# Head pairs split two ways in a chunked RWKV-7 recurrence, half-height state products, and the feed-forward tail moved a chunk later

## The chip, the cores and the metric

The kernel runs on one core of one Trainium2 chip. The metric is the device time of one execution in microseconds (us), as the median of several executions. This program uses one core, so no comparison between the two halves of the chip is needed: every execution quoted here was recorded as a fast one, with its span and its mean granted TensorE clock. The engines are PE (TensorE, matrix products; its weight loads are listed apart as PEld), DVE (VectorE), ACT (ScalarE), POOL (GpSimd) and SP (SyncE, which here only starts transfers).

## The reference, cut to what matters

Four batches of eight heads run a recurrence over 768 steps, with a 40 by 40 state per head. Its output, 3072 tokens of 320 numbers, goes through a feed-forward network (FFN) with a squared ReLU.

```python
B, H, S, D = 4, 8, 768, 40
for t in range(S):                                   # per batch and head
    y[t] = r[t] @ state
    Sa = state @ a[t]
    state = state * w[t][None, :] - outer(Sa, b[t]) + outer(v[t], k[t])
x = y.transpose(0, 2, 1, 3).reshape(3072, 320)
h = np.maximum(x @ w_in, 0.0)                        # w_in  320 x 2048
out = (h * h) @ w_out                                # w_out 2048 x 320
```

## The kernel before

Time is cut into 12 chunks of 64 steps. Inside a chunk the recurrence becomes matrix products: the scaled `a` against the scaled `k` and `b` gives triangular 64 by 64 squares (`PNT`), `r` against the corrected `v` and `b` gives others (`CXT`). `G0` and `M` are two steps of solving the triangular system, `S` is the state that goes to the next chunk, and `ST` is its transpose. `Y` is the chunk's output, and it feeds the FFN of that chunk while the next chunk's recurrence runs. Matrix inputs are bf16, sums are fp32 in PSUM.

All instructions are issued in program order on each engine (`manual_schedule`), so the order of the calls in the loop is the schedule. Three tags: `tr`, one PSUM buffer that every group of transposes shares; `acc`, one buffer for all state and pair products; `hp`, two buffers for the FFN's first product (and for the cumulative sums `cs`).

```python
def transposes(srcs, dst, eng):                       # t_r, t_kb, t_a, t_vm
    trp = ps.tile([128, 8, 128], BF16, name="trp", tag="tr", bufs=1)
    for i, s in enumerate(srcs):
        nc.tensor.transpose(out=trp[:, i, :], in_=s, identity=IDb[:])
    if eng == "act":
        nc.scalar.activation(out=dst, in_=trp[:], func=ACTF.Copy)
    else:
        nc.vector.tensor_copy(out=dst, in_=trp[:])

def scale(self, key, dst, fac):                       # scale_b, scale_k, scale_a
    nc.vector.tensor_tensor(out=dst[:, :, 0:D], in0=self.nat[key][:],
                            in1=fac[:].rearrange("p (h e) -> p h e", e=D), op=ALU.mult)

def state_term(self, bp, acc, lhsT, rhs):             # full height, K = 128
    for q in range(4):
        g = 4 * bp + q
        mm(acc[:, q, 0:160], lhsT[:, g, :], rhs(g), q % 2 == 0)

def g0(self, bp):
    acc = self.acc[bp] = self.new_acc()               # tag "acc", bufs=1
    if not self.first:
        self.state_term(bp, acc, self.AT, ...)        # against ST
    self.pairs(bp, acc, self.PNT[bp], self.VM, not self.first)
    self.evac_m(bp, acc, self.G0)                     # two ACT copies with scale -1

def t_s(self, bp):
    trs = ps.tile([128, 4, 2, 128], BF16, name="trs", tag="tr", bufs=1)
    ...                                               # 8 transposes of S, 2 copies to ST

def t_x(self):
    ...                                               # 6 transposes of Y, tag "tr"
    nc.vector.tensor_copy(out=self.XT[:], in_=trx[:])

def ffn_in(self, jj):                                 # 6 matmuls, then
    ...
    nc.scalar.activation(out=hs[:], in_=hp[:], func=ACTF.Relu)
    nc.vector.tensor_tensor(out=self.Gt[:, 2 * jj:2 * jj + 2, :], in0=hs[:],
                            in1=hs[:], op=ALU.mult)

# the loop (cur: this chunk, nxt: the next, prv: the one before); cut: guards, loads of r and v
for c in range(NCH):
    cur.g0(0); nxt.cs(0); nxt.cs(1); prv.t_x(); nxt.gamp()
    cur.m(0); nxt.t_r(); nxt.scale_b(); nxt.scale_k(); nxt.decays()
    prv.ffn_in(0); prv.ffn_in(1)
    cur.state(0); cur.t_vm(0); nxt.scale_a(); load(c + 2, ...)
    prv.ffn_in(2); cur.g0(1); prv.ffn_in(3)
    cur.t_s(0); cur.m(1); nxt.spread(); prv.ffn_in(4); prv.ffn_in(5)
    cur.state(1); cur.t_vm(1); prv.ffn_in(6); cur.cx(0); prv.ffn_in(7)
    nxt.t_kb(0); cur.y(0); cur.t_s(1); prv.ffn_out(0, 0); cur.cx(1)
    nxt.t_kb(1); prv.ffn_out(0, 1); cur.y(1); nxt.t_a()
    prv.ffn_out(1, 0); nxt.pn(0); prv.ffn_out(1, 1); nxt.pn(1); ch[c + 2].ln()
```

Between two groups of transposes there are nearly always FFN matmuls (`ffn_in`, `ffn_out`) or squares (`cx`). They need nothing from the transposes, so PE has work while another engine empties the one `tr` buffer.

Of the kernel before, what the change touches and what calls it, by code (L numbers as in the profile page):

```python
# [14 lines left out]
def kernel(  # L15
# [11 lines left out]
):  # L27

# [40 lines left out]
    MASK = gl.tile([128, 8, L], BF16, name="MASK")  # L69
    nc.vector.memset(MASK[:], 1.0)  # L70
    for half in range(2):
        nc.gpsimd.affine_select(
            out=MASK[64 * half:64 * half + 64], in_=MASK[64 * half:64 * half + 64],
            pattern=[[0, 8], [1, L]],
            compare_op=ALU.is_gt, fill=0.0, base=0, channel_multiplier=-1,
        )
# [9 lines left out]
    G0s = pair("G0", [128, 2, NI, 64], BF16)  # L86
    Ss = pair("S", [128, NG, 2, 2, 64], BF16)
    STs = pair("ST", [128, NG, 2, 2, D], BF16)
# [5 lines left out]
    def fixed_values(i):  # L94


        for t_ in (Bps[i], Kps[i], Rps[i], Aps[i]):
            nc.vector.memset(t_[:, :, D:64], 0.0)
        for b2 in range(2):
            vrow = 64 - 64 * b2  # L100
            nc.vector.memset(VMs[i][vrow:vrow + 64, b2, :, D:64], 0.0)
            nc.vector.memset(G0s[i][vrow:vrow + 64, b2], 0.0)
        nc.vector.memset(STs[i][:], 0.0)
        nc.vector.memset(Ss[i][:], 0.0)
        nc.vector.memset(Ys[i][:, 640:704], 0.0)

    def load_weights():
        nc.vector.memset(WIN[64:128, 2, :], 0.0)
        nc.gpsimd.dma_start(out=WIN[:, 0:2, :],
                            in_=moe_w_in[0:256, :].rearrange("(g p) f -> p g f", p=128))  # L110
        nc.gpsimd.dma_start(out=WIN[0:64, 2, :], in_=moe_w_in[256:320, :])
        nc.gpsimd.dma_start(out=WOUT[:], in_=moe_w_out.rearrange("(j p) f -> p j f", p=128))
# [42 lines left out]
    class Chunk:  # L155


        def __init__(self, c):
# [6 lines left out]
            self.S, self.ST = Ss[1 - i], STs[1 - i]  # L165
            self.Sn, self.STn = Ss[i], STs[i]
            self.PNT, self.CXT, self.VMT, self.acc = {}, {}, {}, {}
# [24 lines left out]
        def decays(self):  # L192
# [4 lines left out]
            self.GLr = pr.tile([128, 2, W_], BF16, name="GLr", tag="GLr")  # L197
# [5 lines left out]
        def spread(self):  # L203
            for b2 in range(2):
                nc.gpsimd.dma_start(out=self.GLr[0:64 + D, b2, :],  # L205
                                    in_=self.gld[b2:b2 + 1, :].to_broadcast([64 + D, W_]))

        def scale(self, key, dst, fac):
            nc.vector.tensor_tensor(out=dst[:, :, 0:D], in0=self.nat[key][:],
                                    in1=fac[:].rearrange("p (h e) -> p h e", e=D),  # L210
                                    op=ALU.mult)
# [33 lines left out]
        def squares(self, lhs_of, rhs_of, dst):  # L245

            pq = [ps.tile([128, 4, 2, L], FP32, name=f"sq{p}", tag=f"sq{p}", bufs=1)
                  for p in range(2)]
            for q in range(4):
                for b2 in range(2):  # L250
                    for p in range(2):
                        mm(pq[p][:, q, b2, :], lhs_of(q, b2, p), rhs_of(q, b2, p), True)
            dv = dst[:].rearrange("s (q p) b t -> s q p (b t)", p=2)
            for p in range(2):
                nc.vector.tensor_tensor(  # L255
                    out=dv[:, :, p, :], in0=pq[p][:].rearrange("s q b t -> s q (b t)"),
                    in1=MASK[:].rearrange("s (q b) t -> s q (b t)", b=2), op=ALU.mult)

        def pn(self, bp):
            self.PNT[bp] = wk.tile([128, 8, 2, L], BF16, name="PNT", tag="PNT")  # L260
            g0 = 4 * bp
            self.squares(lambda q, b2, p: self.KBT[64 * p:64 * p + D, b2, g0 + q, :],
                         lambda q, b2, p: self.AT[64 * p:64 * p + D, g0 + q,
                                                  64 * b2:64 * b2 + 64],
                         self.PNT[bp])

        def cx(self, bp):
            self.CXT[bp] = wk.tile([128, 8, 2, L], BF16, name="CXT", tag="CXT")
            g0 = 4 * bp
            self.squares(lambda q, b2, p: self.VMT[bp][64 * p:64 * p + D, q, b2, :],  # L270
                         lambda q, b2, p: self.RT[64 * p:64 * p + D, g0 + q,
                                                  64 * b2:64 * b2 + 64],
                         self.CXT[bp])

        def new_acc(self):
            return ps.tile([128, 4, 256], FP32, name="acc", tag="acc", bufs=1)

        def pairs(self, bp, acc, lhs, rhs, started):
            for i in range(8):
                q, p = divmod(i, 2)  # L280
                mm(acc[:, q, 80 * p:80 * p + 80], lhs[:, i].rearrange("s b t -> s (b t)"),
                   rhs[:, :, 8 * bp + i, 0:D], not started and i % 4 == 0)

        def state_term(self, bp, acc, lhsT, rhs):
            for q in range(4):
                g = 4 * bp + q
                mm(acc[:, q, 0:160], lhsT[:, g, :], rhs(g), q % 2 == 0)

        def evac_m(self, bp, acc, dst):
            for b2 in range(2):  # L290
                rows = slice(64 * b2, 64 * b2 + 64)
                src = acc[rows, :, 0:160].rearrange("s q (p b d) -> s q p b d", p=2, b=2)
                nc.scalar.activation(  # L293
                    out=dst[rows, b2, 8 * bp:8 * bp + 8, 0:D].rearrange(
                        "s (q p) d -> s q p d", p=2),
                    in_=src[:, :, :, b2, :], func=ACTF.Copy, scale=-1.0)

        def g0(self, bp):
            acc = self.acc[bp] = self.new_acc()
            if not self.first:  # L300
                self.state_term(bp, acc, self.AT,
                                lambda g: self.ST[:, g].rearrange("k p b d -> k (p b d)"))
            self.pairs(bp, acc, self.PNT[bp], self.VM, not self.first)
            self.evac_m(bp, acc, self.G0)

        def m(self, bp):
            self.pairs(bp, self.acc[bp], self.PNT[bp], self.G0, True)
            self.evac_m(bp, self.acc[bp], self.VM)

        def state(self, bp):  # L310
            if self.last:
                return
            accs = self.new_acc()
            VM, KB, g0 = self.VM, self.KB, 4 * bp
            if not self.first:
                for j in range(2):
                    mm(accs[:, 2 * j:2 * j + 2, 0:160], IDb[:],
                       self.S[:, g0 + 2 * j:g0 + 2 * j + 2, :, :, 0:D].rearrange(
                           "s g b p d -> s (g b p) d"), True)
            for q in range(4):  # L320
                for b2 in range(2):
                    g = g0 + q
                    mm(accs[:, q, 80 * b2:80 * b2 + 80], VM[:, b2, 2 * g:2 * g + 2, :],
                       KB[:, b2, 2 * g:2 * g + 2, 0:D],
                       self.first and q % 2 == 0 and b2 == 0)
            for p in range(2):
                rows = slice(64 * p, 64 * p + D)
                ai = accs[rows, :, 0:160].rearrange("s q (b p d) -> s q b p d", p=2, b=2)
                gv = self.GLr[rows].rearrange("s b (g p d) -> s g b p d", g=NG, p=2)
                nc.vector.tensor_tensor(out=self.Sn[rows, g0:g0 + 4, :, p, 0:D],  # L330
                                        in0=ai[:, :, :, p], in1=gv[:, g0:g0 + 4, :, p],
                                        op=ALU.mult)

        def t_s(self, bp):
            if self.last:
                return
            trs = ps.tile([128, 4, 2, 128], BF16, name="trs", tag="tr", bufs=1)
            g0 = 4 * bp
            for q in range(4):
                for b2 in range(2):  # L340
                    nc.tensor.transpose(  # L341
                        out=trs[:, q, b2, :],
                        in_=self.Sn[:, g0 + q, b2].rearrange("s p d -> s (p d)"),
                        identity=IDb[:])
            for p in range(2):
                rows = slice(64 * p, 64 * p + 64)
                nc.vector.tensor_copy(out=self.STn[rows, g0:g0 + 4, p],
                                      in_=trs[rows, :, :, 64 * p:64 * p + D])

        def t_vm(self, bp):  # L350
            self.VMT[bp] = wk.tile([128, 4, 2, 128], BF16, name="VMT", tag="VMT")
            g0 = 4 * bp
            transposes([self.VM[:, b2, 2 * (g0 + q):2 * (g0 + q) + 2, :]
                        for q in range(4) for b2 in range(2)],
                       self.VMT[bp][:].rearrange("s q b t -> s (q b) t"), "dve")

        def y(self, bp):
            accy = self.new_acc()
            if not self.first:
                self.state_term(bp, accy, self.RT,  # L360
                                lambda g: self.S[:, g, :, :, 0:D].rearrange(
                                    "k b p d -> k p b d"))
            self.pairs(bp, accy, self.CXT[bp], self.KB, not self.first)
            for b2 in range(2):
                rows = slice(64 * b2, 64 * b2 + 64)
                src = accy[rows, :, 0:160].rearrange("s q (p b d) -> s q p b d", p=2, b=2)
                cols = slice(320 * bp, 320 * bp + 320)
                v4 = lambda x: x.rearrange("s (q p d) -> s q p d", q=4, p=2)
# [4 lines left out]
        def t_x(self):  # L373
# [7 lines left out]
            nc.vector.tensor_copy(out=self.XT[:], in_=trx[:])  # L381
            self.Gt = wk.tile([128, NJ, 256], BF16, name="Gt", tag="Gt")

        def ffn_in(self, jj):
# [8 lines left out]
            hs = wk.tile([128, 2, 256], BF16, name="hs", tag="hs", bufs=3)  # L393
# [147 lines left out]
```

## Time and profile before

| | before |
|---|---|
| time, median of 2 runs | 339.66 us (339.51 to 339.81) |
| span in the profile | 338.2 us |
| a steady chunk | 24.35 us |
| PE at work per steady chunk | 21.63 us |
| DVE, ACT at work per steady chunk | 19.43, 14.84 us |
| PE waiting per steady chunk | 2.71 us |

The steady chunk is read from the timeline. The line below appears once in each chunk, so the distance between two of its starts is the time of one chunk. The columns are start, duration of the group, engine, line, operation, output and inputs, count, and in brackets the idle time just before with what ended it.

```profile
136.64 0.89 DVE L185 TENSOR_TENSOR CSE<-cs,lnW 128x320 f32<-128x320 f32 x2 [0.76 <-ACT GAMI L183]
...
160.96 0.89 DVE L185 TENSOR_TENSOR CSE<-cs,lnW 128x320 f32<-128x320 f32 x2 [0.76 <-ACT GAMI L183]
```

The second line starts 24.32 us after the first; over eight chunks, from 87.98 to 282.75 us, the mean is 194.77 / 8 = 24.35 us (seven of them take 24.32 to 24.34, one 24.46).

Over the whole span the page's first part has PE at work 80% of the time, DVE 71% and ACT 53%. The table of windows for the eight steady chunks alone is more useful, since start and end have other limits. The kernel before; the columns are the stretch, its length, then busy time and instructions of PE, PEld, DVE, ACT and POOL, the granted PE clock, the share of the DMA engines and GB/s.

```profile
87.98:282.75 194.77, 173.06 (x2420) 138.87 (x2418) 155.45 (x288) 118.73 (x209) 73.37 (x88) 1.00 0.90 115
```

PE is at work 173.06 of 194.77 us, 89%; it idles 21.71 us, 2.71 us a chunk. The list of PE's waits in the same eight chunks of the same kernel tells whom it waits for (in total, how often, the longest):

```profile
PE trp L145 <- DVE XT L381: 7.3, 8, 0.9
PE acc L152 <- DVE CXT L255: 4.5, 16, 0.4
PE acc L152 <- DVE S_96 L330: 3.9, 4, 1.1
PE acc L152 <- DVE S_97 L330: 3.8, 4, 1.0
PE trp L145 <- DVE VMT L149: 1.6, 8, 0.2
```

These five add up to 21.1 of the 21.71 us. The last of them: PE needs the `tr` buffer that the VMT copy on DVE empties, and it waits 0.2 us each time. The timeline of that place, before:

```profile
146.42 0.61 PE L145 MATMUL trp<-IDb,VM_92 128*128 128x128 bf16 x8
...
147.22 0.99 DVE L330 TENSOR_TENSOR S_96<-acc,GLr 40x320 bf16<-40x320 f32 x2
...
147.96 0.83 PE L389 MATMUL hp<-XT,WIN 128*128 128x256 bf16 x6
148.24 0.69 DVE L149 COPY VMT<-trp 128x1024 bf16<-128x1024 bf16 x1
...
148.99 0.61 PE L145 MATMUL trp<-IDb,KB 128*128 128x128 bf16 x8 [0.20 <-DVE VMT L149]
```

PE writes `tr` at 146.42. DVE first does the two S multiplies, which stand ahead in its order, and then the VMT copy, although the transposes that the copy reads ended at 147.03. So `tr` is free at 148.93. That takes 2.57 us from one group of transposes to the next, but PE fills it with two FFN groups and the squares of `cx(0)` (from 147.62) and idles for only 0.2 us.

In the groups by line, the K scaling takes longer than the B scaling of the same shape (the numbers after the bar are busy time and the mean of one in ns):

```profile
L209 DVE TENSOR_TENSOR Kp_89<-NK,GAMI 128x640 bf16<-128x640 f32 x6 | 11.6, 1939 | 4.7 <-DMA NK<-in_k_dram 4.7
...
L209 DVE TENSOR_TENSOR Bp_90<-NB,GAMI 128x640 bf16<-128x640 f32 x6 | 4.9, 813 | 0.0
```

The K scaling starts just after a POOL multiply (GAMb): in one chunk GAMb starts at 138.49 and lasts 1.63 us, Kp starts at 138.64 and lasts 2.16 us. The Trainium skill (SBUF — State Buffer, Who interferes with whom) says that a DVE instruction with two SBUF inputs contends with a GpSimd instruction that reads SBUF, and that the second to start is blocked for the whole of the first. This trace agrees: 1939 ns against 813 ns for the same shape, and in the chunk quoted Kp ends 0.68 us after GAMb does, which is near the 0.81 us of the unhindered scaling (spans on POOL are rough).

Before 60 us the kernel is bound by loads. The timeline of DVE in chunk 0 of the kernel before:

```profile
41.53 0.83 DVE L209 TENSOR_TENSOR Kp_89<-NK,GAMI 128x640 bf16<-128x640 f32 x1 [4.69 <-DMA NK<-in_k_dram]
...
46.07 0.82 DVE L209 TENSOR_TENSOR Ap_85<-NA,GAMP 128x640 bf16<-128x640 f32 x1 [2.09 <-DMA NA<-in_a_dram]
```

DVE waits 4.69 us for K and 2.09 us for A of chunk 1. In the list of DMA issues, WOUT is read in the same time: 1280.0 KB, and 20.7 us from issue to landing.

### The profile page before, as it was taken

How to read it: one execution, taken by the hardware profiler on the slowest of the kernel's cores; microseconds unless marked ns; L12 is line 12 of the kernel's file. 1: busy time of each engine (PE TensorE's matmuls, PEld its weight loads, DVE VectorE, ACT ScalarE, POOL GpSimd, SP SyncE). 2: the span in 40 equal slices, each digit the busy share in tenths (PEclk: the TensorE clock that was granted, in tenths of full speed). 3: DMA queues.
4: the chain of work that ended last, by engine and by line, in shares of the span. 5: the costliest groups of instructions: out<-in, count | busy, mean ns of one | idle time of the engine just before them, and what ended most of it. 6: DMA issues, size and time to landing. Idle time of an engine off the chain costs nothing.

```text
span 338.2 us, 8736 instructions
## 1 busy us (share of the span) xinstructions
PE 270.3 (80%) x3568; PEld 215.5 (64%) x3568; DVE 238.7 (71%) x450; ACT 180.2 (53%) x313; POOL 114.2 (34%) x143
## 2 busy tenths in 40 slices
PE   0345266989889799799799798898898898898994
PEld 0233155777676677677677776776776777767672
DVE  5417175687887886886986986887886878874740
ACT  2242223564763764765746746746646647637261
POOL 8580531262360460550640640640631623100000
PEclk9999555699999999999999999999999999999999
DMA  9999999099298396495694893992992992200011
GB/s 107 151 185 187 154 183 117 17 151 145 52 170 111 70 163 98 89 176 78 93 166 81 108 162 62 138 134 60 155 138 52 168 130 54 65 21 19 12 33 39
DMA packets 161817, 36.32 MB, mean 107 GB/s; under 512 B 152544, under 2 KB 157664, under 8 KB 161776
## 3 DMA queue, kind: packets, MB, share of 16 engines
q1 hardware_dynamic: 107520, 25.96, 46.8%
q0 software_dynamic: 54256, 9.79, 35.2%
q8 instruction: 28, 0.46, 0.6%
q14 instruction: 13, 0.11, 0.1%
HBM read 32.03 MB, written 3.96 MB: 106 GB/s over the span
## 4 chain that ended last, share of the span: by engine, by line
PE 41%; DVE 17%; ACT 13%; DMA 9%; SPq 9%; issue 9%; DVEq 0%; ACTq 0%
SPq L123 8%; ACT hs L394 8%; PE hp L389 7%; PE acc L152 7%; PE trp L145 6%; DMA out_dram<-osb 5%; DVE CXT L255 4%; DVE S_97 L330 3%; DMA NA<-in_a_dram 3%; DVE S_96 L330 3%; DVE VMT L149 2%; DMA NK<-in_k_dram 2%; DVE Gt L395 2%; DVE XT L381 2%; PE trs L341 2%
## 5 line engine op out<-in xcount | busy, mean ns | idle before, releaser
L389 PE MATMUL hp<-XT,WIN 128*128 128x256 bf16 x576 | 74.5, 273 | 0.7 <-DVE XT L381 0.6
L394 ACT ACTIVATE hs<-hp 128x512 bf16<-128x512 f32 x96 | 54.9, 597 | 24.5 <-PE hp L389 23.8
L194 POOL TENSOR_TENSOR GAMb<-GAMP,NW 128x640 bf16<-128x640 f32 x12 | 19.7, 1646 | 133.1 <-issue 133.1
L389 PEld LDWEIGHTS <-WIN 128*128 128x128 bf16 x576 | 52.7, 98 | 7.0 <-issue 1.4
L395 DVE TENSOR_TENSOR Gt<-hs 128x512 bf16<-128x512 bf16 x96 | 40.5, 422 | 19.3 <-ACT hs L394 17.6
L147 ACT ACTIVATE KBT<-trp 128x1024 bf16<-128x1024 bf16 x24 | 24.6, 1023 | 43.9 <-PE trp L145 43.9
L402 PEld LDWEIGHTS <-Gt 128*128 128x128 bf16 x384 | 35.3, 98 | 12.5 <-issue 0.7
L181 PE MATMUL cs<-lnW,UTI 128*128 128x320 f32 x48 | 19.6, 538 | 7.7 <-ACT lnW L172 7.7
L152 PEld LDWEIGHTS <-PNT 128*128 128x128 bf16 x384 | 19.7, 104 | 8.7 <-DVE S_96 L330 6.6
L145 PE MATMUL trp<-IDb,KB 128*128 128x128 bf16 x192 | 16.2, 233 | 9.3 <-DMA KB<-Kp_88 5.7
L145 PEld LDWEIGHTS <-KB 128*128 128x128 bf16 x192 | 13.1, 104 | 12.4 <-issue 11.6
L185 DVE TENSOR_TENSOR CSE<-cs,lnW 128x320 f32<-128x320 f32 x24 | 10.8, 484 | 13.2 <-ACT GAMI L183 13.2
L293 ACT ACTIVATE G_94<-acc 64x320 bf16<-64x320 f32 x24 | 10.3, 431 | 17.2 <-PE acc L152 17.0
L152 PE MATMUL acc<-KB,CXT 128*128 128x80 bf16 x192 | 13.8, 208 | 6.8 <-DVE CXT L255 6.8
L205 POOL DMA_DIRECT2D GLr<-gld x24 | 14.0, 597 | 10.4 <-DMA gld<-GAMb 7.2
L152 PEld LDWEIGHTS <-KBT 40*128 40x128 bf16 x384 | 9.6, 99 | 12.2 <-issue 10.7
L149 DVE COPY VMT<-trp 128x1024 bf16<-128x1024 bf16 x24 | 16.6, 691 | 0.7
L369 DVE TENSOR_TENSOR Y_100<-acc,GAMP 64x320 bf16<-64x320 f32 x24 | 11.7, 489 | 7.3 <-PE acc L152 7.2
L181 PEld LDWEIGHTS cs<-lnW,UTI 128*128 128x128 f32 x48 | 9.7, 224 | 10.8 <-ACT lnW L172 7.7
L152 PEld LDWEIGHTS <-CXT 128*128 128x128 bf16 x192 | 9.7, 102 | 10.7 <-DVE CXT L255 10.7
L147 ACT ACTIVATE AT<-trp 128x1024 bf16<-128x1024 bf16 x12 | 12.3, 1023 | 7.9 <-PE trp L145 7.9
L369 DVE TENSOR_TENSOR Y_101<-acc,GAMP 64x320 bf16<-64x320 f32 x24 | 11.7, 489 | 6.5 <-PE acc L152 6.4
(336 smaller groups left out, 616.6 us busy)
## 6 DMA issues: line engine op xcount, KB each, us to landing
NW<-in_w_dram SPq DMA_DIRECT2D x24, 160.0 KB, 5.4
NB<-in_b_dram SPq DMA_DIRECT2D x24, 160.0 KB, 6.7
NK<-in_k_dram SPq DMA_DIRECT2D x24, 160.0 KB, 6.3
NA<-in_a_dram SPq DMA_DIRECT2D x24, 160.0 KB, 5.2
out_dram<-osb SPq DMA_DIRECT2D x48, 80.0 KB, 2.1
GLr<-gld POOLq DMA_DIRECT2D x24, 130.0 KB, 5.5
KB<-Bp_90 SPq DMA_DIRECT2D x12, 128.0 KB, 2.4
KB<-Kp_88 SPq DMA_DIRECT2D x12, 128.0 KB, 2.4
```

The lines of the kernel that those rows point to most:

```text
L123: nc.sync.dma_start(out=t_[64 * b2:64 * b2 + 64], in_=src_view(src, c, b2))
L145: nc.tensor.transpose(out=trp[:, i, :], in_=s, identity=IDb[:])
L147: nc.scalar.activation(out=dst, in_=trp[:], func=ACTF.Copy)
L149: nc.vector.tensor_copy(out=dst, in_=trp[:])
L152: nc.tensor.matmul(out=out, lhsT=lhsT, rhs=rhs, start=start, stop=True, skip_group_check=True)
L181: nc.tensor.matmul(out=cs[:, 0:320], lhsT=UTI[:], rhs=self.lnW[:, sl], start=True, stop=True)
L330: nc.vector.tensor_tensor(out=self.Sn[rows, g0:g0 + 4, :, p, 0:D], in0=ai[:, :, :, p], in1=gv[:, g0:g0 + 4, :, p], op=ALU.mult)
L369: nc.vector.tensor_tensor(out=v4(self.Y[rows, cols]), in0=src[:, :, :, b2, :], in1=v4(self.GAMP[rows, cols]), op=ALU.mult)
L389: nc.tensor.matmul(out=hp[:, u, :], lhsT=WIN[:, g, j * 128:(j + 1) * 128], rhs=self.XT[:, g].rearrange("f b t -> f (b t)"), start=(g == 0) ...
L394: nc.scalar.activation(out=hs[:], in_=hp[:], func=ACTF.Relu)
L395: nc.vector.tensor_tensor(out=self.Gt[:, 2 * jj:2 * jj + 2, :], in0=hs[:], in1=hs[:], op=ALU.mult)
L402: nc.tensor.matmul(out=self.op[:], lhsT=self.Gt[:, j, 128 * bp:128 * bp + 128], rhs=WOUT[:, j, :], start=(j == 0), stop=(j == NJ - 1))
```

## The change

The heads are paired by one bit of the head number for k, b and a, and by another bit for r and v. With that, the products that build S put a full 2 by 2 block of useful state where the old layout held two useful quarters; S and ST become dense. The intent has three parts. Fewer operations: 8 S transposes a chunk instead of 16, two ST copies instead of four, one mask and one square instruction where there were two. Half-height state products (`a_s0`, `r_s0`, 40 rows) issued next to the triangular squares, which also use 40 rows. And another order of the loop: the second half of the FFN's output product (`ffn_out(1, *)`) a chunk later, the load of WOUT out of the way of chunk 1's loads. The price is scaling in six pieces instead of three. The XT copy moves from DVE to ACT.

The diff, cut to its core:

```diff
-    Ss = pair("S", [128, NG, 2, 2, 64], BF16)
-    STs = pair("ST", [128, NG, 2, 2, D], BF16)
+    Ss = pair("S", [128, 2, 2, 2, 2, 64], BF16)
 ...
     def scale(self, key, dst, fac):
-        nc.vector.tensor_tensor(out=dst[:, :, 0:D], ...)
+        for z in range(2):                       # two instructions, every other head
+            nc.vector.tensor_tensor(out=dst[:].rearrange(...)[:, :, :, z, 0:D], ...)
 ...
     def squares(self, lhs_of, rhs_of, dst):      # one buffer, one 1024-wide mask
-        for p in range(2):
-            nc.vector.tensor_tensor(out=dv[:, :, p, :], in0=pq[p][:]..., in1=MASK..., op=ALU.mult)
+        nc.vector.tensor_tensor(out=dst[:]..., in0=sq[:]..., in1=MASK[:].to_broadcast(...), op=ALU.mult)
 ...
-    def state_term(self, bp, acc, lhsT, rhs):
-        for q in range(4):
-            mm(acc[:, q, 0:160], lhsT[:, g, :], rhs(g), q % 2 == 0)
+    def a_s0(self, bp):                          # r_s0 alike, RT against S
+        acc = self.accm[bp] = self.new_acc()
+        for g in range(4):
+            q, p = divmod(g, 2)
+            for z in range(2):
+                r = slice(64 * z, 64 * z + D)
+                mm(acc[:, z, 80 * g:80 * g + 80], self.AT[r, 4 * bp + g, :],
+                   self.ST[bp][r, :, q, p, :], g == 0)
 ...
     def t_s(self, bp, nxt):                      # 4 transposes instead of 8, one copy instead of two
+        nc.vector.tensor_copy(out=ST[:]..., in_=trs[:, :, :, 0:D])
 ...
-            nc.vector.tensor_copy(out=self.XT[:], in_=trx[:])
+            nc.scalar.activation(out=self.XT[:], in_=trx[:], func=ACTF.Copy)
```

The new order of the loop, with `old` for the chunk two back (`prv.ffn_out(1, *)` of the order above has become `old.ffn_out(1, *)`):

```python
    cur.a_s0(0); cur.pn(1); cur.g0(0); nxt.cs(0); nxt.cs(1); nxt.gamp(); prv.t_x()
    old.ffn_out(1, 0); cur.m(0); nxt.scale_b(); nxt.scale_k(); nxt.decays()
    old.ffn_out(1, 1); cur.state(0); cur.t_vm(0, "dve"); nxt.scale_a(); load(c + 2, ...)
    prv.ffn_in(0); prv.ffn_in(1); cur.a_s0(1); cur.cx(0); cur.g0(1); prv.ffn_in(2)
    nxt.t_r(); cur.t_s(0, nxt); cur.m(1); nxt.spread(); prv.ffn_in(3); prv.ffn_in(4)
    cur.state(1); cur.t_vm(1, "dve"); [chunk 0 only: load_wout()]
    nxt.t_kb(0); prv.ffn_in(5); cur.r_s0(0); cur.cx(1); cur.y(0); nxt.t_kb(1)
    prv.ffn_in(6); nxt.t_a(); cur.t_s(1, nxt); prv.ffn_in(7); prv.ffn_out(0, 0)
    cur.r_s0(1); nxt.pn(0); cur.y(1); prv.ffn_out(0, 1); ch[c + 2].ln()
```

## The prediction

> **What bounds the kernel now.** The groups by line and the stage table show a steady chunk: it repeats every 24.33 us (S update at 141.53 and 165.86 us in the timeline), of which PE is at work about 21 us, DVE 20, ACT 15. No engine is full. The chain of waits alternates PE, ACT and DVE: every engine works in program order, `acc`, `tr` and `sq` each have one PSUM buffer, so a stage costs its hand-offs: 0.2 us from the last matmul to the evacuation, 0.87 us per negated evacuation pair, 1.02 us per 128x1024 ACT copy, 0.69 us per VMT copy, 0.98 us per S or Y pair. PE idles about 3.3 us a chunk (0.9 for XT, 1.0 for S). Before 60 us the loads bound it: K and A of chunk 1 arrive at 41.5 and 46 us, with WIN and WOUT (20.7 us to landing) in between.
>
> **Removed.** 8 of 16 S transposes (about 56 ns each: 0.45 us PE); state products as half-height pairs (0.5 us PE); two of four ST copies (0.64 us DVE); XT copy from DVE (0.55 us, becoming an estimated 0.8 us on ACT); Gt and mask instructions merged (estimated 0.6 us DVE each). Added: scaling in six pieces instead of three (estimated +0.45 us DVE). Net per chunk: PE -1, DVE -1.8, ACT +0.8. The Trainium skill (TensorEngine Tiling (Array Packing), Key Properties) says a change of tiling mode drains PE; this trace shows 0.2 to 0.26 us before the squares, so batching a_s0/r_s0 with them adds no new drain.
>
> **Moved, and this decides.** By the order of instructions, three uses of the single `tr` bank now stand directly behind one another, where FFN matmuls used to lie between:
> 1. t_r then t_s(0), in front of m(1): PE waits for G0(1)'s evacuation, one hs and RT on ACT: estimated 1.6 us. Before, only the 0.87 us evacuation lay there.
> 2. t_vm(1) then t_kb(0): PE waits for two S multiplies and the VMT copy on DVE: estimated 1.6 us.
> 3. t_kb(1), t_a, t_s(1) behind KBT, hs, KBT, hs, AT on ACT: estimated 1.5 to 1.9 us together.
> Also a_s0(0) waits for pn(0)'s whole mask and Y(1) on DVE (0.8 us), and XT on ACT delays VM(0) and state(0) (0.6 us). The Trainium skill (TensorE: Matmul & The Clock Gate, Architectural detail) calls ACT and DVE strict FIFO; this trace agrees (a matmul starts 0.05 us behind its copy).
>
> Walking the new order by hand with these durations, 20.6 us of work plus 5.5 to 6.5 of stalls give 26 to 27 us a chunk against 24.33; the same walk reproduces the old chunk to 0.1 us. Nine steady chunks cost about +18 to +20 us. WOUT (2.6 MB read) out of chunk 1's loads, and smaller fills, give back an estimated 5 to 8 us before 60 us. The end is about even.
>
> **Predicted:** 351 us, 80% range 337 to 361. Faster by over 2%: 0.14; within 2%: 0.16; slower by over 2%: 0.70.
>
> **What would show it.** The timeline of a middle chunk: period 26 to 27 us; waits of PE's trs and trp matmuls for RT, VMT, KBT and AT of 1 us or more each, where a steady chunk had at most 0.9 us. DVE busy per chunk falls about 2 us. A(1) lands near 33 us, not 46; chunk 1 starts about 53 us, not 60.
>
> **What would make it wrong.** If ACT and DVE run ahead enough that RT and VMT are ready sooner, the stalls shrink, and a chunk could fall to 23 us.

## The result, and the profile after

| | before | after |
|---|---|---|
| time, median of 2 runs | 339.66 us | 357.75 us (357.55 to 357.96) |
| ratio, 95% interval | | 1.0533 (1.0487 to 1.0578) |
| span in the profile | 338.2 us | 356.3 us |
| a steady chunk | 24.35 us | 26.30 us |
| PE at work per steady chunk | 21.63 us | 20.26 us |
| DVE, ACT at work per steady chunk | 19.43, 14.84 us | 17.79, 15.47 us |
| PE waiting per steady chunk | 2.71 us | 6.04 us |

All ratios in this text are the mean time of one kernel's fast runs over the mean time of the other's fast runs of the same rounds, so they are not quite the ratio of the medians that are quoted.

The result is 5% slower. The steady chunk after, from the timeline:

```profile
141.08 0.89 DVE L191 TENSOR_TENSOR CSE<-cs,lnW 128x320 f32<-128x320 f32 x2 [0.53 <-ACT GAMI L189]
...
167.38 0.89 DVE L191 TENSOR_TENSOR CSE<-cs,lnW 128x320 f32<-128x320 f32 x2 [0.53 <-ACT GAMI L189]
```

And the table of windows for its eight steady chunks:

```profile
88.48:298.88 210.40, 162.11 (x2483) 129.81 (x2481) 142.33 (x225) 123.74 (x217) 76.72 (x88) 1.00 0.82 107
```

PE and DVE have less to do and ACT a little more. PE does 10.95 us less work in eight chunks and idles 48.29 us where it idled 21.71. PE's waits in these eight chunks after:

```profile
PE trp L151 <- DVE VMT L155: 13.0, 8, 1.6
PE trs L380 <- ACT RT L153: 11.2, 8, 1.4
PE trs L380 <- ACT AT L153: 8.9, 8, 1.1
PE trp L151 <- ACT KBT L153: 3.7, 8, 0.5
PE acc L158 <- DVE Y_99 L402: 3.0, 4, 0.7
...
```

With the lines left out (the other buffer of Y with 3.0, the two of VM with 2.8 each) they add up to 48.4 us, all of the idle time. The first four, 36.8 us, are all waits for the `tr` buffer: 4.6 us a chunk, where the kernel before had 1.1 (XT and VMT). The timeline of two of them, after:

```profile
148.16 0.61 PE L151 MATMUL trp<-IDb,Rp_87 128*128 128x128 bf16 x8
...
149.10 1.02 ACT L153 ACTIVATE RT<-trp 128x1024 bf16<-128x1024 bf16 x1
...
150.17 0.38 PE L380 MATMUL trs<-IDb,S_96 128*128 128x128 bf16 x4 [1.40 <-ACT RT L153]
...
152.54 0.61 PE L151 MATMUL trp<-IDb,VM_92 128*128 128x128 bf16 x8
...
153.02 0.98 DVE L366 TENSOR_TENSOR S_96<-acc,GLr 40x320 bf16<-40x320 f32 x2
...
154.04 0.69 DVE L155 COPY VMT<-trp 128x1024 bf16<-128x1024 bf16 x1
...
154.78 0.61 PE L151 MATMUL trp<-IDb,KB 128*128 128x128 bf16 x8 [1.63 <-DVE VMT L155]
```

Compare the last four lines with the place shown before. From the VM transposes to the KB transposes it is now 2.24 us, a little less than the 2.57 us of before. DVE is not slower. But PE has nothing to do in it: it ends at 153.15 and stands still for 1.63 us.

The accounts of the span: up to the mark (CSE) of chunk 2, at 87.98 and 88.48 us, the change loses 0.5 us. In eight chunks it loses 210.40 - 194.77 = 15.63 us. From there to the end it is 55.45 us before and 57.42 after, a loss of 2.0 us. Together this is the 18.1 us between the spans.

At the start, the loads do come sooner. The timeline of DVE in chunk 0, after:

```profile
36.76 0.89 DVE L220 TENSOR_TENSOR Kp_89<-NK,GAMI 128x320 bf16<-128x320 f32 x2 [2.46 <-DMA NK<-in_k_dram]
...
39.31 0.89 DVE L220 TENSOR_TENSOR Ap_85<-NA,GAMP 128x320 bf16<-128x320 f32 x2
```

K is scaled 4.8 us sooner than before, and A at 39.31 instead of 46.07 us, without a wait for its load. The loop's first CSE mark comes at 60.15 us against 62.98. Of these 2.8 us nothing is left one chunk later.

### The profile page after: what moved, and what is told of

It reads as the page before. It is cut to its first block, busy times and chain, and to the rows that moved or that the text cites. A ratio compares the mean times of both kernels' runs of the same rounds, so it can differ in the third digit from the quotient of the medians.

```text
span 356.3 us, 8782 instructions
## 1 busy us (share of the span) xinstructions
PE 254.8 (72%) x3656; PEld 202.7 (57%) x3656; DVE 217.2 (61%) x354; ACT 188.2 (53%) x325; POOL 118.6 (33%) x143
## 4 chain that ended last, share of the span: by engine, by line
PE 39%; ACT 26%; DVE 14%; DMA 7%; issue 7%; SPq 5%; ACTq 0%; DVEq 0%
PE acc L158 10%; PE hp L422 9%; DMA NK<-in_k_dram 7%; PE trp L151 7%; SPq L129 5%; ACT hs L429 4%; PE sq L158 3%; ACT KBT L153 3%; ACT AT L153 3%; ACT G_94 L332 3%; ACT RT L153 3%; PE trs L380 2%; DVE VMT L155 2%; ACT VM_92 L332 2%; DVE CSE L191 2%
## 5 line engine op out<-in xcount | busy, mean ns | idle before, releaser
L429 ACT ACTIVATE hs<-hp 128x512 bf16<-128x512 f32 x96 | 56.0, 595 | 32.7 <-PE hp L422 31.7
L431 DVE TENSOR_TENSOR Gt<-hs 128x1024 bf16<-128x1024 bf16 x48 | 33.1, 690 | 57.9 <-ACT hs L429 57.9
L422 PEld LDWEIGHTS <-WIN 128*128 128x128 bf16 x576 | 53.6, 99 | 6.0 <-issue 0.6
L266 DVE TENSOR_TENSOR PNT<-sq,MASK 128x1024 bf16<-128x1024 f32 x24 | 29.3, 1223 | 17.4 <-PE sq L158 10.2
L266 DVE TENSOR_TENSOR CXT<-sq,MASK 128x1024 bf16<-128x1024 f32 x24 | 29.2, 1218 | 1.6 <-PE sq L158 1.6
L151 PEld LDWEIGHTS <-KB 128*128 128x128 bf16 x192 | 13.4, 105 | 25.9 <-issue 25.9
L385 DVE COPY ST<-trs 128x320 bf16<-128x320 bf16 x22 | 7.1, 325 | 26.0 <-PE trs L380 26.0
L212 POOL DMA_DIRECT2D GLr<-gld x24 | 19.9, 846 | 4.4 <-DVE Gt L431 1.9
L158 PEld LDWEIGHTS <-PNT 128*128 128x128 bf16 x384 | 18.4, 104 | 3.2 <-issue 1.1
L140 POOL DMA_DIRECT2D VM_93<-in_v_dram x12 | 10.2, 863 | 22.0 <-PE trp L151 22.0
L140 POOL DMA_DIRECT2D VM_92<-in_v_dram x12 | 10.0, 841 | 21.1 <-PE trp L151 20.9
L380 PE MATMUL trs<-IDb,S_96 128*128 128x128 bf16 x48 | 5.0, 231 | 14.8 <-ACT RT L153 8.1
```

Source lines behind the costliest of these rows:

```text
L140: nc.gpsimd.dma_start(out=VMs[c % 2][row:row + 64, b2, :, 0:D], in_=src_view(v, c, b2))
L158: nc.tensor.matmul(out=out, lhsT=lhsT, rhs=rhs, start=start, stop=True, skip_group_check=True)
L266: nc.vector.tensor_tensor(out=dst[:].rearrange("s x g b t -> s (x g b) t"), in0=sq[:].rearrange("s x g b t -> s (x g b) t"), in1=MASK[:].t ...
L422: nc.tensor.matmul(out=hp[:, u, :], lhsT=WIN[:, g, j * 128:(j + 1) * 128], rhs=self.XT[:, g].rearrange("f b t -> f (b t)"), start=(g == 0) ...
L429: nc.scalar.activation(out=self.hs[:, u:u + 2], in_=hp[:], func=ACTF.Relu)
L431: nc.vector.tensor_tensor(out=self.Gt[:, 2 * jj - 2:2 * jj + 2, :], in0=self.hs[:], in1=self.hs[:], op=ALU.mult)
```

## The experiments

The theory: the operations that the change removes are a gain, and the loss comes from the order alone, from uses of the single `tr` buffer put directly behind one another. The rival: the operations are to blame (half-height products, instructions in two pieces, the wide masks and squares, XT on ACT). A further rival for part of it is the load of WOUT and the moved FFN tail. All eleven kernels gave correct results. The kernel before had medians of 339.28, 339.38 and 339.27 us in the three sessions. The time of a steady chunk in what follows is the mean distance of the CSE marks in the timeline, over eight chunks. No run puts all of the old operations into the new order, or the new ones into the old order.

| kernel | median us (range) | ratio to before (95%) | steady chunk, us |
|---|---|---|---|
| before | 339.66 | 1 | 24.35 |
| after | 357.75 | 1.0533 | 26.30 |
| e1_tr_after_m | 351.22 (350.46 to 352.96) | 1.0366 (1.0333 to 1.0399) | 25.80 |
| e2_late | 339.54 (338.85 to 340.28) | 1.0005 (0.9985 to 1.0026) | 24.48 |
| e3_both | 320.12 (317.89 to 321.27) | 0.9425 (0.9385 to 0.9464) | 22.72 |
| b1_adjacent | 365.15 (364.45 to 365.31) | 1.0756 (1.0739 to 1.0772) | 26.84 (26.53 to 27.16) |
| e4_wout_early | 363.72 (363.17 to 364.46) | 1.0719 (1.0700 to 1.0738) | 26.31 |
| e5_tail_back | 394.34 (392.05 to 396.09) | 1.1597 (1.1550 to 1.1643) | 28.66 to 30.33 |
| e6_xt_k | 318.51 (317.16 to 319.42) | 0.9382 (0.9354 to 0.9409) | 22.64 |
| e7_cs_first | 311.07 (310.44 to 313.13) | 0.9176 (0.9143 to 0.9210) | 21.98 |
| e8_before_wout | 334.05 (333.90 to 334.15) | 0.9840 (0.9821 to 0.9859) | 24.35 |
| e9_a_later | 302.68 (301.43 to 303.82) | 0.8914 (0.8891 to 0.8937) | 21.36 |
| e10_xt_dve | 358.08 (357.41 to 359.60) | 1.0555 (1.0531 to 1.0579) | 26.50 |

### e1_tr_after_m: the RT transposes away from the S transposes

```diff
 cur.g0(1); prv.ffn_in(2)
-nxt.t_r()
 cur.t_s(0, nxt); cur.m(1)
+nxt.t_r()
 nxt.spread(); prv.ffn_in(3); prv.ffn_in(4)
```

> The changed kernel with one move: the eight transposes of r go behind m(1) instead of in front of t_s(0). Same instructions, same counts. Theory (order: a single transpose bank used back to back): the 1.40 us wait of the S transposes for the RT copy in front of m(1) goes, part of it returns as a wait of m(1) for the G0 copy, so 1.0 to 1.4 us less per chunk, in all 344 to 349 us. Rival (the new operations themselves, the dense S, merged masks, split scaling, are slower): no change, 356 to 359 us.

Measured: 351.22 us, and a steady chunk of 25.80. That is outside the expected range, so it is a miss: faster than the kernel after, but by only 0.5 us a chunk, though the wait of 1.40 us for RT is gone. The timeline of this kernel tells why:

```profile
171.48 0.61 PE L151 MATMUL trp<-IDb,Rp 128*128 128x128 bf16 x8 [0.65 <-DVE ST L385]
...
172.12 1.02 ACT L153 ACTIVATE RT<-trp 128x1024 bf16<-128x1024 bf16 x1 [0.37 <-PE trp L151]
173.67 0.69 DVE L431 TENSOR_TENSOR Gt<-hs 128x1024 bf16<-128x1024 bf16 x1 [2.24 <-ACT hs L429]
...
174.28 0.98 DVE L366 TENSOR_TENSOR S<-acc,GLr 40x320 bf16<-40x320 f32 x2
```

Only the short products of `m(1)` now stand between `t_s(0)` and `t_r`, so the RT transposes wait for the ST copy (0.65 us here; in three of the eight chunks they wait for the load of r instead, by at most 0.7). These two waits add up to 5.3 us in the eight chunks, 0.66 us a chunk, and that is most of what the move fails to bring. The RT copy now also stands on ACT ahead of the two hs of the FFN, and the Gt square on DVE waits 2.24 us for them, where it waited 1.50 us in the kernel after. But the S multiply behind it starts 0.3 us after its products end in both kernels, and PE's wait for VMT stays at 1.63 us, so no cost of this shows.

### e2_late: FFN matmuls back between the later uses

```diff
-nxt.t_kb(0); prv.ffn_in(5)
+prv.ffn_in(5); nxt.t_kb(0)
 cur.r_s0(0); cur.cx(1); cur.y(0); nxt.t_kb(1); prv.ffn_in(6)
-nxt.t_a(); cur.t_s(1, nxt); prv.ffn_in(7); prv.ffn_out(0, 0)
+prv.ffn_in(7); nxt.t_a(); prv.ffn_out(0, 0); cur.t_s(1, nxt)
```

> The changed kernel with the second half of the loop reordered, no other edit: one FFN block between t_vm(1) and t_kb(0), two between t_kb(1) and t_a, half a head of ffn_out between t_a and t_s(1). Theory (order): the waits of 1.63 (t_kb for VMT), 0.46 (t_a for KBT) and 1.11 us (t_s for AT) shrink to about 0.95, 0 and 0.45, so 1.6 to 1.9 us less per chunk, in all 338 to 343 us. Rival (operations): no change, 356 to 359 us.

Measured: 339.54 us, a ratio of 1.0005, with a chunk of 24.48 us. Three calls moved by one or two places give back the whole loss. In this kernel's PE waits, VMT falls from 1.63 to 1.0 us a chunk, KBT from 0.46 to 0.2 and AT from 1.11 to 0.2, while the wait for RT (untouched) stays at 1.40. These differences add up to 1.8 us, and the chunk is 26.30 - 24.48 = 1.82 us shorter.

### e3_both: the same instructions, all three places spread out

```diff
 e2_late, and:
-cur.g0(1); prv.ffn_in(2); nxt.t_r(); cur.t_s(0, nxt); cur.m(1); nxt.spread(); prv.ffn_in(3)
-prv.ffn_in(4); cur.state(1); cur.t_vm(1, "dve")
+cur.g0(1); prv.ffn_in(2); cur.t_s(0, nxt); cur.m(1); nxt.spread(); prv.ffn_in(3)
+nxt.t_r(); cur.state(1); prv.ffn_in(4); cur.t_vm(1, "dve")
```

> Both reorderings together, with t_r one step later (behind an FFN block, before the state product) and one FFN block moved between the state product and t_vm(1). Theory (order): the two gains add, 2.6 to 3.2 us less per chunk, period near 23.4 us, in all 324 to 332 us, so faster than the kernel before (339.7). Rival (operations): 356 to 359 us; a weak form of the rival, in which the operations cost something too, lands between 340 and 350.

Measured: 320.12 us, 5.75% faster than the kernel before. That is a miss on the good side: 324 to 332 us and a chunk near 23.4 us were expected. The chunk is 3.58 us shorter than in the kernel after, where e1_tr_after_m and e2_late gained 0.50 and 1.82 alone: here an FFN group stands ahead of the RT transposes, and the new wait of e1_tr_after_m does not come; another now stands ahead of the VM transposes, and the wait for VMT falls to 0.2 us, from 1.0 in e2_late. The table of windows and PE's waits for its eight steady chunks:

```profile
82.92:264.68 181.76, 164.69 (x2483) 130.96 (x2481) 141.85 (x225) 123.13 (x217) 76.89 (x88) 1.00 0.95 124
```

```profile
PE acc L158 <- DVE Y L402: 5.9, 8, 0.7
PE acc L158 <- ACT VM L332: 5.6, 8, 0.7
PE trp L151 <- ACT KBT L153: 1.9, 8, 0.2
PE trp L151 <- DVE VMT L155: 1.4, 8, 0.2
PE trs L380 <- ACT AT L153: 1.3, 8, 0.2
```

The numbers of instructions on PE, DVE and ACT in these chunks are those of the kernel after (2483, 225, 217). Only their order differs, and the time falls by 37.6 us. The waits for `tr` are 0.2 us or less. The wait for RT is gone. This decides between theory and rival: the operations of the change do not cause the loss, since with all of them and another order the kernel is faster than before, and the order is what cost the time. That the operations by themselves are a gain is not shown by this run, because the WOUT load and the FFN tail have moved as well. What speaks for it is PE's work per chunk: e9_a_later, below, has a chunk of 21.36 us, and PE alone had 21.63 us of work in a chunk of the kernel before.

### b1_adjacent: the same fault put into the old kernel

```diff
 cur.state(1); cur.t_vm(1)
+nxt.t_kb(0)
 prv.ffn_in(6); cur.cx(0); prv.ffn_in(7)
-nxt.t_kb(0)
 cur.y(0)
```

> The kernel before, with old operations throughout, in which only t_kb(0) moves up to stand directly behind t_vm(1), as in the changed kernel; the three blocks that lay between (two of FFN, one of squares) follow it. Theory (order): a wait of about 1.6 us for the VMT copy appears at t_kb(0), of which the old waits for the masks (0.4 and 0.3 us) give back some: 0.9 to 1.6 us more per chunk, in all 349 to 356 us. Rival (operations): the old operations can't lose from this, 338 to 342 us.

Measured: 365.15 us. One call moved in the old kernel, none of the new operations, and it loses 25.9 us to the old kernel of the same session. The sign is as the theory has it; the size is a miss, more than was expected. Most of it is waiting: where the clock stays at 1.00 a chunk takes 26.54 us, 2.2 more than before. The VMT wait is 1.96 us instead of 0.2, and the waits for the masks, which had been expected to shrink, grow from 0.6 to 1.0 us. The rest of the steady loss is the clock. First PE's line in the timeline, then the stretch just after it in the table of windows:

```profile
184.25 0.44 PE L145 MATMUL trp<-IDb,KB 128*128 128x128 bf16 x5 [1.96 <-DVE VMT L149]
```

```profile
185.00:188.20 3.20, 3.20 (x31) 2.16 (x29) 1.45 (x3) 1.66 (x3) 1.14 (x2) 0.50 1.78 142
```

PE idles 1.96 us for the VMT copy, and less than a microsecond later the granted clock (the third number from the right) is 0.50 for some 3 us, where it was 1.00 in the gap. In such a chunk the kernel pays the wait and a stretch at half the clock, 27.0 us in the mean instead of 26.5. The same wait of 1.96 us stands in all eight chunks, and the clock fell in five of them. The clock records of this trace show a pattern: each low stretch lasts 3.41 us, and they begin whole multiples of 3.41 us apart (130.17, 157.48, 184.79, 212.09, 239.40 us). In the five chunks the whole gap lies within one such step, the one before the fall; in the other three it is divided over two steps, with at most 1.74 us in one. No run tests this by moving the gap. The kernel after, with gaps of 1.63 us, shows a clock of 1.00 over all its steady chunks.

### e4_wout_early and e8_before_wout: the load of WOUT, undone and done alone

```diff
 e4_wout_early, on the kernel after:
 load_win()
+load_wout()
 ...
-if c == 0:
-    load_wout()

 e8_before_wout, on the kernel before:
-(the load of WOUT, behind that of WIN)
 ...
 cur.t_vm(1)
+if c == 0:
+    load_wout()
```

> The changed kernel with the load of WOUT put back where the kernel before had it, behind WIN, in the middle of the first loads. My prediction said that moving it away gives back 5 to 8 us before 60 us; the trace showed the first chunk ending only about 2 us earlier. If that small gain is all from WOUT: 359.5 to 361 us. If the prediction's mechanism was right but something else took the rest: 362 to 366 us. If the load's place means nothing: 357 to 358.5 us.

> The kernel before with one part of the change alone: WOUT is loaded in chunk 0 behind t_vm(1), no longer among the first loads. In the changed kernel the same move was worth 6.0 us (363.7 to 357.8). Theory (the move shortens the wait for the k and a loads of chunk 1, whatever the loop's order): 4 to 7 us less, 332.5 to 335.5 us. If the old order can't use it: 338.5 to 340 us.

Measured: 363.72 us, 6.0 us above the kernel after, with the same steady chunk (26.31); and 334.05 us, 5.2 us below the kernel before of its session, with the same steady chunk (24.35). The two agree: moving this load is worth 5 to 6 us and leaves the steady chunk as it was. The timeline of DVE in e4_wout_early shows the wait:

```profile
42.12 0.89 DVE L220 TENSOR_TENSOR Kp<-NK,GAMI 128x320 bf16<-128x320 f32 x2 [6.72 <-DMA NK<-in_k_dram]
```

The wait for K is 6.72 us here and 2.46 in the kernel after. It also tells why the first mark of the kernel after came only 2.8 us sooner than before's: without the WOUT move it would come at 65.51 us (e4_wout_early), 2.5 us later than before's 62.98. Chunk 0 too pays for the new order: in e1_tr_after_m, the kernel after with one call moved, the mark comes at 57.70 us, 2.45 us sooner than in the kernel after.

### e5_tail_back: the FFN tail back in its own chunk

```diff
-old.ffn_out(1, 0)
 cur.m(0) ...
-old.ffn_out(1, 1)
 ...
 cur.y(1); prv.ffn_out(0, 1)
+prv.ffn_out(1, 0); prv.ffn_out(1, 1)
```

> The changed kernel with the second half of the FFN output product back at the end of its own chunk, as in the kernel before; nothing else. Theory: the state product in the first half of a chunk waits for a chain on ACT (G0 copy, GAMI, GAMP, XT, VM) that the two FFN blocks of 1.1 us each now cover; moved back, they hide the 0.74 us wait for Y at the chunk's end but open a hole of about 3 us there, so 1.0 to 1.5 us more per chunk, 367 to 374 us, and more if the hole drops the granted clock. Rival (the late tail is what costs): faster than 357.8 us, 345 to 353.

Measured: 394.34 us, 36.6 above the kernel after, again more than was expected. The move of the FFN tail is a gain of the change, and a large one in this order. Without it the start of the chunk (G0, M, S, each needing the evacuation of the one before) has nothing to fill PE with. A line of the timeline, and two neighbouring chunks in the table of windows:

```profile
213.31 0.43 PE L158 MATMUL acc<-S,IDb 128*128 128x320 bf16 x2 [2.73 <-ACT VM L332]
```

```profile
120.66:149.32 28.66, 20.54 (x314) 16.40 (x312) 17.88 (x28) 15.46 (x27) 9.62 (x11) 1.00 0.79 97
149.32:179.63 30.31, 22.19 (x314) 17.55 (x312) 18.02 (x28) 15.46 (x27) 9.65 (x11) 0.94 0.72 93
```

The waits alone make it 28.66 us a chunk, 2.4 more than the kernel after and already more than the 1.0 to 1.5 that were expected. In six of the eight chunks the clock fell too (0.94 in the mean), with the same 314 matmuls taking 22.19 instead of 20.54 us, and the chunk took 30.2 to 30.3. Of the 28.6 us that the eight chunks lose against the kernel after, about 19 are waits and about 10 the clock. The gap of 2.73 us is in the other two chunks as well, but there a border of the 3.41 us steps divides it, with at most 1.90 us on one side.

### e10_xt_dve: one term of the prediction by itself

```diff
 kernel after, with:
-            nc.scalar.activation(out=self.XT[:], in_=trx[:], func=ACTF.Copy)
+            nc.vector.tensor_copy(out=self.XT[:], in_=trx[:])
```

> The changed kernel with the XT copy back on DVE, nothing else. My prediction counted 0.6 us of stall per chunk for XT on ACT. If the term was right as a cost: 350.5 to 352.5 us. If the k scaling, standing still behind the POOL product, holds the S multiply anyway, so that the earlier VM copy buys nothing: 356 to 358.5 us.

Measured: 358.08 us, as the kernel after within its spread (357.41 to 359.60 against 357.55 to 357.96). The prediction counted 0.6 us a chunk for XT on ACT, because it delays VM(0) and with it `state(0)`. PE does show that wait in the kernel after (0.7 us for VM). As a whole, the move to ACT cost nothing. But the run does not take the wait away alone: it puts XT's 0.55 us back into DVE's order. Its steady chunk is 0.20 us longer than in the kernel after, and PE waits 0.4 us for VMT and 0.24 for S in place of the 0.7 for VM; its start makes up for that (chunk 2's mark at 86.59 instead of 88.48 us). The timeline of e10_xt_dve, where the wait for VM is gone:

```profile
141.45 1.69 POOL L200 TENSOR_TENSOR GAMb<-GAMP,NW 128x640 bf16<-128x640 f32 x1 [12.19 <-issue]
141.66 2.23 DVE L220 TENSOR_TENSOR Kp<-NK,GAMI 128x320 bf16<-128x320 f32 x2
...
142.14 0.43 PE L158 MATMUL acc<-S,IDb 128*128 128x320 bf16 x2
...
143.82 0.98 DVE L366 TENSOR_TENSOR S<-acc,GLr 40x320 bf16<-40x320 f32 x2
```

PE starts `state(0)` at 142.14 without that wait, but DVE takes the result only at 143.82, because the K scaling stands ahead of it in DVE's order and is held up by the POOL multiply. Counted from the chunk's CSE mark, the S multiply starts 4.23 us on (139.59 to 143.82) and 3.99 us on in the kernel after (141.08 to 145.07). Behind the wait for VM stood a second one, for DVE, and that one decided.

### e6_xt_k: XT on DVE, and the K scaling behind the VMT copy

```diff
 e3_both, with XT as in e10_xt_dve, and:
-nxt.scale_b(); nxt.scale_k(); nxt.decays()
+nxt.scale_b(); nxt.decays()
 old.ffn_out(1, 1); cur.state(0); cur.t_vm(0, "dve")
+nxt.scale_k()
 nxt.scale_a()
```

> On top of both reorderings (320 us): the XT copy back on DVE and the scaling of k behind the first state update and the VMT copy. Theory: XT on ACT holds the VM copy back by 0.7 us, and the k scaling, which stands still behind the POOL product, holds the S multiply; without both the state product starts about 0.6 us earlier in each chunk, period 22.0 to 22.2, in all 313 to 316 us. Rival (that stretch is bound by PE or by the FFN blocks): 319 to 321 us.

Measured: 318.51 us, and a chunk of 22.64 against 22.72. A miss: the wait at `state(0)` went, but a new one came. The K pieces now stand later in DVE's order, ahead of the A scaling, a Gt square and the CXT mask, and the ST copy comes late behind all of these. PE waits for it 0.81 us, as the timeline of this kernel shows:

```profile
158.50 0.61 PE L151 MATMUL trp<-IDb,Rp 128*128 128x128 bf16 x8 [0.81 <-DVE ST L385]
```

### e7_cs_first and e9_a_later: two more calls moved

```diff
 e7_cs_first, on e6_xt_k:
-cur.a_s0(0); cur.pn(1); cur.g0(0); nxt.cs(0); nxt.cs(1); nxt.gamp()
+nxt.cs(0); nxt.cs(1); cur.a_s0(0); cur.pn(1); cur.g0(0); nxt.gamp()
 ...
-prv.ffn_out(0, 1); ch[c + 2].ln()
+ch[c + 2].ln(); prv.ffn_out(0, 1)

 e9_a_later, on e7_cs_first:
-nxt.scale_k(); nxt.scale_a()
+nxt.scale_k()
 ...
 cur.t_s(0, nxt)
+nxt.scale_a()
```

> On top of that: the cumulative sum of the next chunk goes in front of the first state product, where PE waits 0.74 us for the Y evacuation, and the logarithm in front of the last FFN output block. Theory: the wait is covered and the chain GAMI, CSE, GAMP starts 1 us earlier, period 21.2 to 21.8, in all 304 to 311 us. Rival: the chunk is at PE's own work (about 20.6 us and four drains) and the gain is under 0.3 us per chunk, 311 to 316 us.

> On the fastest version so far (311 us): the scaling of a moves behind the first S transposes. There t_r waits 0.83 us in each chunk for the ST copy, which stands on DVE behind the scaling of k and a, a Gt square and a mask; without the two pieces for a (0.89 us) the copy comes in time. Theory: 0.6 to 0.8 us less per chunk, 303 to 306 us. Rival (the wait reappears at once behind the Gt square, where the scaling then stands): 309 to 312 us.

Measured: 311.07 us and 302.68 us, each just past an edge of its range, the one above 304 to 311 and the other below 303 to 306. The first fills PE's wait for Y(1) at the start of the chunk with the two cumulative sums, which need only the logarithms. The second takes the A scaling out of DVE's order ahead of the ST copy. The last one is the fastest version: 10.9% faster than the kernel before. The table of windows for nearly six of its steady chunks:

```profile
74.00:200.00 126.00, 121.36 (x1820) 96.62 (x1819) 107.16 (x173) 89.00 (x156) 58.16 (x66) 1.00 1.00 130
```

PE is at work 121.36 of 126.00 us, 96%, against 89% in the kernel before and 77% in the kernel after.

## Why the prediction was right

The time, 357.75 us, lies inside the range (337 to 361), and slower by over 2% was called with a chance of 0.70. The point, 351, was 6.75 us low. Step by step:

1. **What bounds the kernel: hand-offs, with no engine full.** Right. PE's list of waits explains nearly all of its idle time in both kernels (21.1 of 21.7 us and all of 48.3), and reordering the same instructions (e3_both) moved 37.6 us. PE's idle time before was put too high, 3.3 us a chunk where 2.71 are measured, and its work too low, about 21 where it is 21.63.
2. **What the operations save.** PE -1 us, DVE -1.8, ACT +0.8 a chunk were predicted. Measured: PE 21.63 to 20.26, -1.37; DVE 19.43 to 17.79, -1.64; ACT 14.84 to 15.47, +0.63. The batching of state products and squares adds no drain: the page of the Trainium skill cited in the prediction (TensorEngine Tiling (Array Packing), Key Properties) says that a change of mode drains PE, and the trace of the kernel after shows one gap of 0.21 to 0.26 us between weight loads (PEld) ahead of a state product and its squares and none between them (146.72 and 146.84 us). There are three such gaps a chunk, where the kernel before had four.
3. **The three places where `tr` is used twice in a row.** Right in place, and in size but for one: the wait for KBT was to be 1 us or more and is 0.46. RT 1.6 us predicted, 1.40 measured; VMT 1.6 and 1.63; KBT and AT 1.5 to 1.9 together, and 0.46 + 1.11 = 1.57. Y(1) 0.8 and 0.75. With VM, 0.6 and 0.70, the sum is 6.05 us, where 5.5 to 6.5 was predicted, and the chunk is 26.30 us, where 26 to 27 was. The experiments then show these as causes and not only as waits: e2_late takes 1.8 us out of three of them and the chunk gets 1.82 us shorter; b1_adjacent puts one into the old kernel and that gets slower.
4. **"XT on ACT delays VM(0) and state(0) (0.6 us)".** Mis-sized: the wait is there with 0.7 us, but moving XT back to DVE gains nothing (e10_xt_dve, 358.08 us), since the S multiply stands behind the K scaling on DVE. The sum of waits comes out right in spite of it, because such a sum counts every idle time of PE once, whichever of several causes ended it; it does not tell what taking one cause away is worth.
5. **"WOUT out of chunk 1's loads, and smaller fills, give back an estimated 5 to 8 us before 60 us", and "chunk 1 starts about 53 us".** This is the term that failed. The load alone is worth what was said, 5.2 and 6.0 us (e8_before_wout, e4_wout_early). But the first chunk runs the new order too, and that costs it 2.5 us (62.98 to 65.51, with WOUT as before). The net gain at the loop's first mark is 2.8 us, chunk 1's first state product is at 56.9 instead of 60.0 us, and by chunk 2 it is 0.5 us behind. A(1) has landed at 37.6 us, not near 33, and is scaled at 39.3. The steady loss had been counted from the second chunk on, and the gain of the start on top of it, as if the first chunk were free of it.
6. **"The end is about even."** Mis-sized: it is 2.0 us longer (57.42 against 55.45 us).

The steady loss itself was well sized: +18 to +20 us were predicted for nine chunks, and 15.63 us in eight and 3.3 in chunk 1 (from 2.8 us ahead to 0.5 behind) make 18.9. Against an assumed gain of 6.5 us at the start (the middle of the estimate) stood 2.8, which is 3.7 us, and the end adds 2.0: 5.7 of the 6.75 us. The last microsecond lies in the prediction itself, whose terms, taken at their middles, give 352 and not 351. What remains open: how the 2.0 us at the end are made up was not tested by a run of its own, and the waits of chunk 0 were not taken apart further.

What none of this foresaw is that the same operations, put in another order, would be faster than both kernels: the prediction treated the order as a part of the change. It names the right cause, but it does not say that the cause can be taken away. Nor did it put a price on the moved FFN tail, which in this order is worth 36.6 us (e5_tail_back).

## What to carry to other kernels

Where every engine works in program order, a PSUM buffer that exists once needs independent PE work between two of its uses, as long as the evacuation and everything that stands ahead of it in the evacuating engine's order; count that before you judge a change by the operations that it removes. A change that bundles fewer operations with a new order should be taken apart by running the same instructions in another order, because an order that gives back all of the gain can hide a good one. A wait on PE is worth moving only if nothing behind it would wait anyway: look at what the next engine does at that moment.

## What the Trainium skill lacked or had wrong

- TensorE: Matmul & The Clock Gate, "Why this matters for your kernels", asks for no PE gaps over about 3 us between bursts of matmuls. Here a wait of 1.96 us was followed by a granted clock of 0.50 for some 3 us in five of eight chunks (b1_adjacent), and one of 2.73 us went with a fallen clock in six of eight (e5_tail_back, 0.94 in the mean of such a chunk), while waits of 1.63 us and less in every chunk left it at 1.00 (the kernel after). Where the clock stayed up behind the longer waits, a border of the 3.41 us steps of the clock records divided them, with at most 1.90 us in one step. The section "A second HAM failure mode: psum-queue depth-cycling" of the same page does say that frequent short idle times can do it, without a length.
- TensorEngine Tiling (Array Packing), Key Properties, says that a mode switch drains PE, but not what it costs. Here a gap of 0.21 to 0.26 us between weight loads stands ahead of the 40-row products, and one of only 0.05 us behind them, on the way back to 128 rows; in PE's matmuls no idle time shows at either. That the gap is the drain is inferred.
- None of the pages read gives what the second of two groups of transposes costs when both use the same PSUM buffer. Here it was 1.40 us behind a 128x1024 copy on ACT and 1.63 us behind two S multiplies and a 128x1024 copy on DVE, and 0.2 us where matmuls lay between them. Perfetto Trace Analysis, Matmuls, advises rotating independent groups through PSUM banks, without a cost.
